# Two gated linear-attention blocks on one core: A's reciprocals spread through a DRAM scratch, and part of A's row work moved

## The chip, the core and the metric

The kernel runs on one core of one Trainium2 chip. A core has five engines that run side by side, each with its own queue of instructions that it works through in order: TensorE (PE, matrix products, with a weight load before each matmul, shown as PEld), VectorE (DVE), ScalarE (ACT), GpSimd (POOL) and SyncE (SP, which here issues transfers). Matmuls write to PSUM, a small memory of eight banks per partition; everything else lies in SBUF, 128 partitions wide, or in DRAM. An engine that needs another's result waits on a semaphore, and what is queued behind the waiting instruction waits too.

The metric is the time of one execution on the device in microseconds, lower is better.

## The reference

The input x has 2048 rows of 640 features. Two attention blocks, A and B, with weights of their own work on the same x, and a gate mixes them:

```
qkv = x @ wqkv                        # 640 -> 3 * 640; 32 heads of 20 features
phi = lambda t: where(t > 0, t + 1, exp(t)) + 1e-6
pq, pk = phi(q), phi(k)
kv  = einsum("bhsd,bhse->bhde", pk, v)
z   = einsum("bhsd->bhd", pk)
num = einsum("bhqd,bhde->bhqe", pq, kv)
den = einsum("bhqd,bhd->bhq", pq, z)[..., None] + 1e-6
o   = num / den ;  block = o @ wo
g   = sigmoid((x * gate_w).sum(-1, keepdims=True))
out = g * A(x) + (1 - g) * B(x)
```

All inputs and the output are bf16.

## The kernel before

The kernel never forms v. Since kv = pk' x wv, it makes G = x' pk (640 x 640), multiplies it by the weights of v, keeps the blocks on the diagonal that belong to the same head, and multiplies by wo: the result is one matrix M for each block, and the output is pq_A M_A + pq_B M_B, if each row of pq is first multiplied, head by head, by gate / den.

The stages, in the order in which TensorE meets them (times of the profiled execution):

- k of A and half of A's q, then the other half of q (up to 52.7 us). A chunk of k has 128 rows, ten matmuls of 320 columns (`k_mm`, L210); a unit of q has 128 features and 1024 rows, ten matmuls of 512 columns (`q_unit`, L259). Behind each, `phi` (L197) takes an exp on ACT (L200), a min and add on DVE (L203) and an add and max on DVE (L207), which frees the PSUM bank pair. The q rows are kept transposed in `pqT[b]`, as five feature tiles of 128 partitions by 2048 rows; tile m holds every fifth feature from m on, so that partition p of each tile belongs to head p // 4.
- `g_all` (A from 52.7 to 74.1 us, B from 122.1 to 143.5 us): one feature tile of G by `g_pass`, the denominators and their reciprocals by `rec_pass`, and the other four tiles of G by a scheme of Strassen's kind (`g_strassen`, L323): seven products of 16 matmuls (`g_prod`, L318), in two PSUM bank pairs that are partly accumulated over and partly read out between the products by `add` (L335, L366).
- k of B (74.1 to 99.0 us) in 16 chunks, with A's kv and M_A (`kv_a`, `m_a`) between them. M_A's rows go to a DRAM scratch, `ma_dram`, and come back as one transfer on SP's queue. `p_diff` stands here too, after chunks 3, 6, 9 and 12: `D3` = first half of A's scaled q rows minus the second half, a quarter of the rows of all five tiles at a time, 128x1280 elements.
- q of B (99.0 to 122.1 us): ten units. Behind the fourth and behind the last stands a difference of pk rows (`k_sum(1, 1)`, `k_sum(1, 2)`, 128x2560 on DVE).
- `g_all` for B, then M_B and the output product, again in Strassen's manner, in eight pairs of row blocks (`Pair`), up to the end at 189.7 us. `D3` is read from 151.8 us on.

The reciprocals, in detail. `rec_pass` (L468) makes the denominators as a tile whose 128 partitions are 4 groups of 256 rows by 32 heads, for each half of the rows. DVE adds eps and multiplies by the gate (L477, 128x256) and takes the reciprocal (L482, 128x256) into `rT`, once for each half. The q rows want it with 4 partitions for each head and all 2048 rows along the free dimension. `norm_spread` (L518) does that with eight matmuls of a 0/1 matrix (`spread`, L524, four for each half) into two PSUM bank pairs, which ACT copies into `R` (L529, two copies). `scale(b, m)` (L534, L537) then multiplies feature tile m of `pqT[b]` by `R`, 128x2048 bf16 on DVE. In `g_strassen` the spreading stands behind the second product, and the five multiplications stand one or two at a time between the read-outs of the later products.

From `k_chunk(0, ST - 2)` on, the order of the instructions on each engine is the order in which the program writes them (`tc.manual_schedule()`); before that a scheduler sets it. The Tile framework adds the waits, by the regions that instructions read and write.

Of the kernel before, what the change touches and what calls it, by code (L numbers as in the profile page):

```python
# [8 lines left out]
P = 128  # L9
FP32 = mybir.dt.float32  # L10
BF16 = mybir.dt.bfloat16
ACT = mybir.ActivationFunctionType
ALU = mybir.AluOpType

S, D, H = 2048, 640, 32
# [7 lines left out]
TW = 4  # L23
# [5 lines left out]
RB = 256  # L29
SH = S // 2  # L30
# [3 lines left out]
def kernel(  # L34
# [11 lines left out]
    nc = tc.nc  # L46
# [7 lines left out]
    scratch = ctx.enter_context(tc.tile_pool(name="scratch", bufs=1, space=bass.MemoryType.DRAM))  # L54
# [12 lines left out]
    def ps(name, slot=None):  # L67

        return ps_raw(name, slot).bitcast(FP32).rearrange("p (b n) -> p b n", b=2)
# [4 lines left out]
    pqT = [persist.tile([P, DT, S], BF16, name=f"pqT{b}") for b in "AB"]  # L74
# [10 lines left out]
    R = persist.tile([P, 2, 4, RB], BF16, name="R")  # L85
    ones = persist.tile([P, H], BF16, name="ones")
    gwr = persist.tile([P, DT, H], BF16, name="gwr")
    D3 = persist.tile([P, DT, SH], BF16, name="D3")
    hc, ic = ST // 2, 2 * P

    def flat(t, pattern, inner, at=0):
        n = hc * inner
        return t[:].rearrange(pattern)[:, at * n:(at + 1) * n].rearrange("p (i n) -> p i n", i=hc)
# [4 lines left out]
    TK = [{k: flat(pqT[1], "p c s -> p (c s)", HF, k - 1) for k in (1, 2, 3, 4)},  # L98
          {k: flat(xT, "p c s -> p (c s)", HF, k - 2) for k in (2, 3, 4)}]
    ma_dram = scratch.tile([D, D], BF16, name="ma_dram")  # L100
    lift = persist.tile([P, 1], FP32, name="lift")
    TM = [persist.tile([P, DT, HF], BF16, name="TM0")] + [None] * 3
    ge = [persist.tile([P, 2 * RB], FP32, name=f"ge{b}") for b in "AB"]
# [30 lines left out]
    for n in range(1, NB):  # L134
        for c in range(DT):
            nc.sync.dma_start_transpose(
                out=xT[:, c, n * HB:(n + 1) * HB], in_=x2[n * HB:(n + 1) * HB, c * P:(c + 1) * P]
# [4 lines left out]
    for r in range(4):  # L142
        rows = slice(32 * r, 32 * r + 32)
        nc.gpsimd.tensor_copy(out=I4[rows], in_=ident[rows, rows])
    nc.gpsimd.tensor_copy(
        out=spread[:].rearrange("p (h t) -> p h t", t=TW), in_=I4[:, :, None].to_broadcast([P, H, TW])
    )
    nc.gpsimd.memset(maskE[:], 1.0)
    for sign, base in ((1, 0), (-1, Dh - 1)):
        nc.gpsimd.affine_select(  # L150
            out=maskE[:], in_=maskE[:], pattern=[[-sign * Dh, WB[0] // Dh], [0, Dh]],
# [3 lines left out]
    for r in range(4):  # L155
        rows = slice(32 * r, 32 * r + 32)
        for sign, base in ((1, 0), (-1, Dh - 1)):
            nc.gpsimd.affine_select(
                out=E4[rows], in_=E4[rows], pattern=[[sign, D]],
# [121 lines left out]
    def g_pass(b, c, slot):  # L281

        pt = ps(f"g{'AB'[b]}", slot)
        for i in range(ST):
            for hf in range(2):
                g_mm(c, i, hf, pt)
        for hf in range(2):
            nc.scalar.copy(out=GT[hf][:, c, :], in_=pt[:, hf, 0:HF])
# [17 lines left out]
    def k_sum(b, k):  # L306

        b11, b12 = [pk[:, 0:hc, n * HF:(n + 1) * HF] for n in range(2)]
        b21, b22 = [pk[:, hc:ST, n * HF:(n + 1) * HF] for n in range(2)]
        t = TK[b]  # L310
        left, right = {1: lambda: (b12, b11), 2: lambda: (b22, t[1]), 3: lambda: (b22, b12), 4: lambda: (b21, t[2])}[k]()
        add_rows(t[k], left, right, ALU.subtract)

    def g_prod(pt, left, right, first):

        for i in range(hc):
            for n in range(2):
                nc.tensor.matmul(  # L318
                    pt[:, n, 0:HF], lhsT=left[:, i, n * P:(n + 1) * P], rhs=right[:, i, :],
                    start=(first and i == 0), stop=(i == hc - 1), skip_group_check=not first,  # L320
                )

    def g_strassen(b, norm):  # L323

        x11, x12 = [xn[:, k:k + hc, 0:ic] for k in (0, hc)]
        x22 = xn[:, hc:ST, ic:2 * ic]
        b11 = pk[:, 0:hc, 0:HF]
        b21, b22 = [pk[:, hc:ST, n * HF:(n + 1) * HF] for n in range(2)]
        lo, hi = GT

        def temp(name):
            return work.tile([P, 2, HF], FP32, tag="osb", name=name, bufs=3)

        def add(dst, pt, sb):
            nc.vector.tensor_tensor(out=dst, in0=pt[:, :, 0:HF], in1=sb[:], op=ALU.add)  # L335

        even, odd = ps("gs0", 0), ps("gs1", 1)
        g_prod(even, x11, b11, True)
        p1 = temp("p1")
        nc.scalar.copy(out=p1[:], in_=even[:, :, 0:HF])  # L340
        g_prod(odd, SX[2], TK[b][2], True)
        u2 = temp("u2")
        add(u2[:], odd, p1)
        k_sum(b, 4)
        norm()
        g_prod(even, x12, b21, False)
        nc.scalar.copy(out=lo[:, 0:2, :], in_=even[:, :, 0:HF])
        scale(b, 0)
        scale(b, 1)
        g_prod(odd, SX[3], TK[b][3], False)  # L350
        u3 = temp("u3")
        add(u3[:], odd, p1)
        if b == 0:
            x_sum(4)
        else:
            scale(b, 2)
        even = ps("gs0", 0)
        g_prod(even, SX[1], TK[b][1], True)
        add(hi[:, 2:4, :], even, u3)
        scale(b, 3 if b else 2)  # L360
        g_prod(odd, x22, TK[b][4], False)
        add(lo[:, 2:4, :], odd, p1)
        scale(b, 4 if b else 3)
        g_prod(even, SX[4], b22, False)
        for n in range(2):
            nc.vector.tensor_tensor(out=hi[:, n, :], in0=even[:, n, 0:HF], in1=u2[:, n], op=ALU.add)  # L366
        if b == 0:
            scale(b, 4)

    def z_rows(b):  # L370

# [96 lines left out]
    def rec_pass(b, zsel, slot):  # L468

        pt = ps(f"den{'AB'[b]}", slot)  # L470
        for h in range(2):
            by_group(pt[:, 0, h * RB:(h + 1) * RB], zsel, pqT[b], h)
        rts = []
        for h in range(2):
            part = slice(h * RB, (h + 1) * RB)
            d1 = work.tile([P, RB], FP32, tag="d1", name="d1", bufs=1)
            nc.vector.scalar_tensor_tensor(  # L477
                out=d1[:], in0=pt[:, 0, part], scalar=EPS, in1=ge[b][:, part], op0=ALU.add, op1=ALU.mult
            )
            rT = work.tile([P, RB], BF16, tag="rT", name="rT")  # L480
            with nc.allow_low_precision(reason="a fp32 reciprocal, stored as the bf16 that multiplies bf16"):
                nc.vector.reciprocal(out=rT[:], in_=d1[:])  # L482
            rts.append(rT)
        return rts

    def add_rows(dst, a, b, op):
        nc.vector.tensor_tensor(out=dst, in0=a, in1=b, op=op)  # L487

    def p_diff(rows):

        up = slice(SH + rows.start, SH + rows.stop)
        add_rows(D3[:, :, rows], pqT[0][:, :, rows], pqT[0][:, :, up], ALU.subtract)

    def p_sums(rows, ks=(1, 2, 4)):

# [22 lines left out]
    def norm_spread(b, rts, slots):  # L518

        pts = [ps(f"ex{'AB'[b]}", s) for s in slots]  # L520
        for h in range(2):
            for j in range(4):
                rows = slice(32 * j, 32 * j + 32)
                nc.tensor.matmul(  # L524
                    pts[j // 2][:, j % 2, h * RB:(h + 1) * RB], lhsT=spread[rows, :], rhs=rts[h][rows, :],
                    start=True, stop=True,
                )
        for jj in range(2):
            nc.scalar.copy(  # L529
                out=R[:, :, 2 * jj:2 * jj + 2, :].rearrange("p h j n -> p j h n"),  # L530
                in_=pts[jj][:].rearrange("p j (h n) -> p j h n", n=RB),
            )

    def scale(b, m):  # L534

        rec = R[:].rearrange("p h j n -> p (h j n)")
        nc.vector.tensor_tensor(out=pqT[b][:, m, :], in0=pqT[b][:, m, :], in1=rec, op=ALU.mult)  # L537
# [106 lines left out]
    def q_pass(b, units):  # L644

        units = list(units)
        q_unit(b, *units.pop(0))
        if b == 0:
            gate_pass()
        zr = z_rows(b)  # L650
        for k in range(2):
            if b == 0:
                x_sum(1 + k)
            q_unit(b, *units.pop(0), b == 0)
        zsel = z_pass(b, zr)
        for k, (m, h) in enumerate(units):
            if b == 0 and k < 2:
                if k:
                    x_sum(3)
                else:  # L660
                    k_sum(0, 2)
            q_unit(b, m, h, b == 0)
            if b == 1 and k == 0:
                k_sum(1, 1)
        if b == 1:
            k_sum(1, 2)
        return zsel

    def g_all(b, zsel):

        g_pass(b, DT - 1, 1)
        k_sum(b, 3)
        rts = rec_pass(b, zsel, 2)
        g_strassen(b, lambda: norm_spread(b, rts, (2, 3)))


    with tc.manual_schedule():
# [12 lines left out]
    for n in range(1, NB):  # L690
        nc.sync.dma_start(
            out=xn[:, n * CB:(n + 1) * CB, :], in_=x2[n * HB:(n + 1) * HB, :].rearrange("(q p) d -> p q d", p=P)
# [11 lines left out]
    with tc.manual_schedule():  # L704
# [10 lines left out]
        for i in range(ST):  # L715
            k_chunk(1, i)
            if i > 3 and i % 2 == 0:
                m_a(i // 2 - 2)
            if i == 1:
                kv_a()  # L720
                wv[1] = load_w(1, "v", nc.sync)
            if i in (3, 6, 9, 12):
                r0 = (i - 3) // 3 * RB
                p_diff(slice(r0, r0 + RB))
        load_wo(1, nc.sync)
        t1 = wpool.tile([P, hc, HF], BF16, tag="wk", name="T1")
        TK[1][1] = t1[:]
# [109 lines left out]
```

## Time and profile before

| | |
|---|---|
| time, median of 3 runs | 190.9 us (190.49 to 191.43) |
| the profiled execution | 191.42 us, span 189.7 us |
| TensorE busy | 184.0 us, 97% of the span |
| VectorE busy | 152.7 us, 80% |
| ScalarE busy | 70.5 us, 37% |
| transfers | 15.63 MB, mean 82 GB/s |
| a reciprocal (L482, 128x256) | 1.75 us, four of them |
| a multiplication by R (L537, 128x2048) | 1.22 us, ten of them |
| a difference of q rows into D3 (L487, 128x1280) | 0.815 us, four of them |
| an R copy from PSUM (L529, 128x1024) | 1.01 us, four of them |

The span is the time from the first to the last instruction of one execution that a hardware profiler recorded; the time of an execution is a little longer than its span. A line of the timeline gives the start, the duration, the engine, the line of the program, the operation with the tiles that it writes and reads, and the number of instructions merged into it; in brackets stands the idle time of the engine before it and what ended it. The chain of work that ended last is followed back from the last instruction, at each step to what released it. DVE's records overlap a little: the next instruction starts some 0.08 us before the listed end of the one in front.

### The profile page before, as it was taken

Reading aid. Unit: us, or ns where it says so; the run is one execution under the profiler, and the core shown is the slowest. Engines: PE = TensorE matmul, PEld = TensorE weight load, DVE = VectorE, ACT = ScalarE, POOL = GpSimd, SP = SyncE. Lnnn points to the kernel's source line nnn. Section 1 sums busy time; section 2 is a strip of 40 time slices with the busy share of each in tenths; the row PEclk is TensorE's granted clock in tenths of the full one; section 3 lists DMA queues with packets and bytes.
Section 4 is the critical chain, followed back from the end, with each engine's and each line's share of the span. In section 5 each row is a group of like instructions: output and inputs, shape, how many; then the busy total and the mean of one; then the engine's idle time right before and its main releaser. Section 6 shows DMA issues by size and latency. Waiting matters only on the chain.

```text
span 189.7 us, 3630 instructions
## 1 busy us (share of the span) xinstructions
PE 184.0 (97%) x1490; PEld 124.7 (66%) x1497; DVE 152.7 (80%) x244; ACT 70.5 (37%) x99; POOL 8.6 (5%) x23
## 2 busy tenths in 40 slices
PE   8799999999999999999999999999999999999992
PEld 3566657765567677877775555576777776777771
DVE  1378968899898999789886689799999989787553
ACT  2055446455953500357672445412401611111110
POOL 8900000000000000000000000000000000000000
PEclk9999999999999999999999999999999999999999
DMA  5976438993050000241116600000000003212112
GB/s 181 324 143 87 88 78 273 343 224 101 2 173 0 3 0 0 42 166 32 54 40 218 146 5 0 0 0 3 0 0 3 3 0 108 99 65 77 69 69 73
DMA packets 19802, 15.63 MB, mean 82 GB/s; under 512 B 9546, under 2 KB 19658, under 8 KB 19786
## 3 DMA queue, kind: packets, MB, share of 16 engines
q1 hardware_dynamic: 18922, 14.59, 28.5%
q10 hardware_dynamic: 864, 0.82, 1.3%
q8 instruction: 11, 0.18, 0.4%
q14 instruction: 5, 0.04, 0.1%
HBM read 10.00 MB, written 3.44 MB: 71 GB/s over the span
## 4 chain that ended last, share of the span: by engine, by line
PE 93%; DMA 3%; DVE 1%; ACTq 0%; issue 0%; ACT 0%; DVEq 0%
PE gs L318 16%; PE kB L210 11%; PE qB L259 11%; PE kA L210 11%; PE qA L259 7%; PE ox L548 6%; PE oy L548 5%; PE oz L548 5%; PE qA L270 4%; DMA xn<-in_A_x_dram 3%; PE ow L548 3%; PE gB L291 2%; PE gA L291 2%; DVE osb L553 1%; PE mA L441 1%; PE mid L402 1%
## 5 line engine op out<-in xcount | busy, mean ns | idle before, releaser
L210 PEld LDWEIGHTS <-xT 128*128 128x128 bf16 x320 | 31.0, 98 | 12.3 <-DVE xT L195 0.4
L203 DVE TENSOR_SCALAR e<-e 128x640 bf16<-128x640 bf16 (+1 forms) x52 | 18.8, 361 | 9.6 <-ACT e L200 9.0
L210 PE MATMUL kB<-wkB,xT 128*128 128x320 bf16 x160 | 23.0, 299 | 0.0
L210 PE MATMUL kA<-wkA,xT 128*128 128x320 bf16 x160 | 22.6, 299 | 0.0
L259 PE MATMUL qB<-xT,wqB 128*128 128x512 bf16 x97 | 22.0, 379 | 0.2
L200 ACT ACTIVATE e<-kB 128x640 bf16<-128x640 f32 x16 | 11.3, 704 | 18.8 <-PE kB L210 17.5
L259 PEld LDWEIGHTS <-wqB 128*128 128x128 bf16 x100 | 11.6, 118 | 9.6 <-issue 0.3
L200 ACT ACTIVATE e<-kA 128x640 bf16<-128x640 f32 x16 | 11.1, 704 | 13.6 <-PE kA L210 13.6
L200 ACT ACTIVATE e<-qB 128x1024 bf16<-128x1024 f32 x10 | 10.2, 1024 | 13.2 <-PE qB L259 10.7
L207 DVE SCALAR_TENSOR_TENSOR pk<-kA,e 128x640 bf16<-128x640 f32 x16 | 13.2, 824 | 1.7
L207 DVE SCALAR_TENSOR_TENSOR pk<-kB,e 128x640 bf16<-128x640 f32 x16 | 13.2, 824 | 1.7
L200 ACT ACTIVATE e<-qA 128x1024 bf16<-128x1024 f32 x10 | 10.2, 1024 | 10.6 <-PE qA L259 5.2
L259 PE MATMUL qA<-xT,wqA 128*128 128x512 bf16 x58 | 13.5, 380 | 0.1
L207 DVE SCALAR_TENSOR_TENSOR pqTB<-qB,e 128x1024 bf16<-128x1024 f32 x10 | 12.2, 1224 | 1.0
L318 PEld LDWEIGHTS <-S 128*128 128x128 bf16 x96 | 9.4, 98 | 3.6
L318 PEld LDWEIGHTS <-xn 128*128 128x128 bf16 x96 | 9.1, 98 | 4.0 <-issue 0.4
L592 ACT COPY u<-ox 128x320 f32<-128x320 f32 x8 | 3.4, 426 | 21.9 <-PE ox L548 21.9
L259 PEld LDWEIGHTS <-wqA 128*128 128x128 bf16 x60 | 6.9, 118 | 5.6 <-issue 0.3
L548 PEld LDWEIGHTS <-xT 128*128 128x128 bf16 x85 | 8.0, 98 | 3.1 <-DVE xT L487 0.2
L548 PEld LDWEIGHTS <-pqTA 128*128 128x128 bf16 x85 | 7.9, 98 | 2.9 <-issue 0.2
L548 PEld LDWEIGHTS <-pqTB 128*128 128x128 bf16 x80 | 7.8, 98 | 3.0
L576 ACT COPY p1s<-ox 128x320 f32<-128x320 f32 x8 | 3.4, 426 | 16.6 <-PE ox L548 16.6
(121 smaller groups left out, 287.7 us busy)
## 6 DMA issues: line engine op xcount, KB each, us to landing
out_dram<-osb SPq DMA_DIRECT2D x14, 160.0 KB, 1.8
xn<-in_A_x_dram SPq DMA_DIRECT2D x3, 640.0 KB, 7.2
wqA<-in_A_wqkv_dram SPq DMA_DIRECT2D x1, 800.0 KB, 6.5
wvA<-in_A_wqkv_dram SPq DMA_DIRECT2D x1, 800.0 KB, 11.0
wkB<-in_B_wqkv_dram SPq DMA_DIRECT2D x1, 800.0 KB, 5.8
wqB<-in_B_wqkv_dram SPq DMA_DIRECT2D x1, 800.0 KB, 4.5
wvB<-in_B_wqkv_dram SPq DMA_DIRECT2D x1, 800.0 KB, 4.6
MA<-ma_dram SPq DMA_DIRECT2D x1, 800.0 KB, 4.4
```

Of the source, the lines that this page charges most:

```text
L200: nc.scalar.activation(out=e[:], in_=src, func=ACT.Exp)
L203: nc.vector.tensor_scalar(e[:], e[:], 1.0, EPS, op0=ALU.min, op1=ALU.add)
L207: nc.vector.scalar_tensor_tensor(out=dst, in0=src, scalar=1.0 + EPS, in1=e[:], op0=ALU.add, op1=ALU.max)
L210: nc.tensor.matmul(pt[:, hf, 0:HF], lhsT=xT[:, c, i * P:(i + 1) * P], rhs=wk[b][:, c, hf * HF:(hf + 1) * HF], start=(c == 0), stop=(c == D ...
L259: nc.tensor.matmul(pt[:, u, :], lhsT=mixed(wq[b][:, c, :], m), rhs=xT[:, c, n * HB:(n + 1) * HB], start=(c == 0), stop=(c == DT - 1),)
L270: nc.tensor.matmul(pt[:, u, :], lhsT=mixed(wq[b][:, c, :], m + u), rhs=xT[:, c, n * HB:(n + 1) * HB], start=(c == 0), stop=(c == DT - 1),)
L291: nc.tensor.matmul(pt[:, hf, 0:HF], lhsT=xn[:, i, c * P:(c + 1) * P], rhs=pk[:, i, hf * HF:(hf + 1) * HF], start=(i == 0), stop=(i == ST - 1),
L318: nc.tensor.matmul(pt[:, n, 0:HF], lhsT=left[:, i, n * P:(n + 1) * P], rhs=right[:, i, :], start=(first and i == 0), stop=(i == hc - 1), s ...
L402: nc.tensor.matmul(pt[:KG, hf, j * KG:(j + 1) * KG], lhsT=wv[b][:, c, (4 * hf + j) * KG:(4 * hf + j + 1) * KG], rhs=GT[hf][:, c, j * KG:(j ...
L548: nc.tensor.matmul(dst, lhsT=left[:, c, r0:r0 + P], rhs=right[:, c, :], start=(first and c == 0), stop=(c == DT - 1), skip_group_check=not ...
L576: nc.scalar.copy(out=self.p1s[:], in_=self.at("x"))
L592: nc.scalar.copy(out=self.u2[:], in_=self.at("x"))
```

## The change

Four things are changed, all of them for block A's q rows; B's reciprocals are spread as before.

- A's reciprocals `rT` (128x256 bf16, two halves) are stored to a new DRAM scratch, `r_dram`, by SP's queue, as soon as each half is there. `norm_load` then loads `R` from it in four transfers, one for each partition of the four that belong to a head (32 partitions, 8 runs of 512 bytes in each). A's eight spreading matmuls and two PSUM copies go.
- In A's `g_strassen` the multiplications of tiles 0, 1 and 2 now stand where those of tiles 2, 3 and 4 stood; the place behind the fourth product, where 0 and 1 stood, is empty.
- The multiplications of A's tiles 3 and 4 stand in B's q pass, behind the sixth and the eighth of its ten units.
- `p_diff` takes one feature tile with all 1024 rows at a time (128x1024). Tiles 0, 1 and 2 stand in B's k chunks, behind chunks 4, 8 and 12; tiles 3 and 4 stand in B's q pass, behind the seventh and the ninth unit.

```diff
+    r_dram = scratch.tile([2, P, RB], BF16, name="r_dram")
...
         nc.scalar.copy(out=lo[:, 0:2, :], in_=even[:, :, 0:HF])
-        scale(b, 0)
-        scale(b, 1)
+        if b == 1:
+            scale(b, 0)
+            scale(b, 1)
...
-        scale(b, 3 if b else 2)
+        scale(b, 3 if b else 0)
         g_prod(odd, x22, TK[b][4], False)
         add(lo[:, 2:4, :], odd, p1)
-        scale(b, 4 if b else 3)
+        scale(b, 4 if b else 1)
...
         if b == 0:
-            scale(b, 4)
+            scale(b, 2)
...
             rts.append(rT)
+            if b == 0:
+                nc.sync.dma_start(out=r_dram[h], in_=rT[:])
...
-    def p_diff(rows):
-
-        up = slice(SH + rows.start, SH + rows.stop)
-        add_rows(D3[:, :, rows], pqT[0][:, :, rows], pqT[0][:, :, up], ALU.subtract)
+    def p_diff(c):
+
+        add_rows(D3[:, c, :], pqT[0][:, c, 0:SH], pqT[0][:, c, SH:S], ALU.subtract)
...
+    def norm_load():
+
+        src = r_dram[:].rearrange("a (j h) n -> h a j n", h=H)
+        for u in range(TW):
+            nc.sync.dma_start(out=R[u::TW], in_=src)
...
             q_unit(b, m, h, b == 0)
             if b == 1 and k == 0:
                 k_sum(1, 1)
+            if b == 1 and k in (2, 4):
+                scale(0, k // 2 + 2)
+            if b == 1 and k in (3, 5):
+                p_diff(k // 2 + 2)
...
         rts = rec_pass(b, zsel, 2)
-        g_strassen(b, lambda: norm_spread(b, rts, (2, 3)))
+        if b == 0:
+            norm_load()
+        g_strassen(b, lambda: norm_spread(b, rts, (2, 3)) if b else None)
...
-            if i in (3, 6, 9, 12):
-                r0 = (i - 3) // 3 * RB
-                p_diff(slice(r0, r0 + RB))
+            if i in (4, 8, 12):
+                p_diff(i // 4 - 1)
```

## The prediction

> **What bounds the kernel now.** I read the page first, for the engine shares and the chain of work that ended last; then that chain in order of time around the two places that the change touches; then VectorE's timeline there; then the waits, the DMA issues and the granted clock.
>
> The page's first part and its chain:
>
> ```profile
> PE 184.0 (97%) x1490; PEld 124.7 (66%) x1497; DVE 152.7 (80%) x244; ACT 70.5 (37%) x99; POOL 8.6 (5%) x23
> PE 93%; DMA 3%; DVE 1%; ACTq 0%; issue 0%; ACT 0%; DVEq 0%
> ```
>
> TensorE is the bound: 97% busy, 93% of the chain. A saving counts only if it takes time out of TensorE's queue, and a delay elsewhere counts as soon as TensorE waits for it. The chain in order of time where A's reciprocals are spread, and at the same place for B:
>
> ```profile
> 58.29 4.45 PE gs L318 x32
> 62.74 0.40 PE exA L524 x8
> 63.15 10.97 PE gs L318 x80
> ...
> 122.11 4.35 PE gB L291 x32
> 126.45 1.21 PE denB L174 x40
> 127.66 4.45 PE gs L318 x32
> 132.11 0.40 PE exB L524 x8
> 132.51 10.97 PE gs L318 x80
> ```
>
> The spreading matmuls (exA, exB) stand on the path for 0.40 us each. Only A's go. Now VectorE (DVE) in B's q pass and behind it, until B's reciprocals are done (columns: start us, duration us; in brackets the idle time before):
>
> ```profile
> 110.25 0.43 DVE L203 TENSOR_SCALAR e<-e 128x1024 bf16<-128x1024 bf16 x1 [0.37 <-ACT e L200]
> ...
> 118.88 0.43 DVE L203 TENSOR_SCALAR e<-e 128x1024 bf16<-128x1024 bf16 x1 [0.40 <-ACT e L200]
> ...
> 123.20 0.43 DVE L203 TENSOR_SCALAR e<-e 128x1024 bf16<-128x1024 bf16 x1 [0.40 <-ACT e L200]
> 123.73 1.22 DVE L207 SCALAR_TENSOR_TENSOR pqTB<-qB,e 128x1024 bf16<-128x1024 f32 x1
> 124.87 1.48 DVE L487 TENSOR_TENSOR xT<-pk,T 128x2560 bf16<-128x2560 bf16 x1
> 126.27 1.48 DVE L487 TENSOR_TENSOR xT<-pk 128x2560 bf16<-128x2560 bf16 x1
> 127.71 0.42 DVE L477 SCALAR_TENSOR_TENSOR d<-denB,geB 128x256 f32<-128x256 f32 x1
> 128.17 1.75 DVE L482 RECIPROCAL rT<-d 128x256 bf16<-128x256 f32 x1
> 129.96 0.42 DVE L477 SCALAR_TENSOR_TENSOR d<-denB,geB 128x256 f32<-128x256 f32 x1
> 130.41 1.75 DVE L482 RECIPROCAL rT<-d 128x256 bf16<-128x256 f32 x1
> ```
>
> What to see: from 123.20 to the second reciprocal's end (130.41 + 1.75 = 132.16) DVE runs without a gap worth naming, and exB, which needs that reciprocal, stands on TensorE at 132.11. The slack there is nil. Whatever DVE gets to do in B's q pass beyond its idle time ends up as a TensorE wait in front of exB's second half.
>
> **The change part by part.** Durations are of the profiled execution: span 189.7, time 191.42 us, at the upper end of the three runs (median 190.9). I make the sum as a difference and put it on the median.
>
> 1. *A's spreading matmuls go.* Eight matmuls, 0.40 us by the chain. Bounds: columns alone, at kB's rate (10 matmuls of 320 columns in 1.36 us), are 2 x 256 x 0.425 ns = 0.22 us, four row groups side by side; the whole stretch is 0.40. I take 0.40, since the stretch's waits go too. The two R copies on ACT (2 x 1.01 us) also go; ACT waits for TensorE behind them (9.4 us before its next exp), so they are worth nothing.
>
> 2. *A's R by DRAM.* Two stores of 64 KB and four loads of 128 KB on SP's queue. SP issues nothing between 52.8 and 78.4 us (weights wqB, then wvB) and DMA is idle there, so nothing is queued behind them that suffers: wvB still waits for TensorE's kvA. The second store waits for the reciprocal that ends at 62.80. A store of this kind to the scratch and the dependent load behind it took 1.76 us (the last evacuation of M_A's rows ends at 98.68, the load of MA is issued at 100.44), so the R loads issue from 64.6, at 0.35 us each. Landing, lower end by bytes: MA and woB, issued one behind the other, brought 1,600 KB in 7.6 us, so 512 KB in 2.5: 67.1. Upper end by packets: gcol, 640 packets, took 4.9 us; 1,024 packets of 512 B then take 7.8: 72.4. I take 69, nearest the byte end, because these packets are like those of the weights. [...]
>
> 3. *Three multiplications (L537) later in A's Strassen product, two of them moved on.* On DVE, u3 and SX4 now come without two multiplications in front, so nothing there is later. The first multiplication comes behind the add that in the old trace starts at 69.81; shifted by 0.40 and with 0.74 for the add, at 70.15. With R at 69 it waits for nothing. The multiplication behind the last add stands where it stood, so DVE enters B's k chunks with the same lag behind TensorE. Cost 0. If R is late, what waits behind the multiplication is the add into GT (0.82) that frees the bank of B's first k chunk, due at 73.55: TensorE is held from R > 73.55 - 0.82 - 1.14 = 71.6 on; at R = 72.4 the cost is 0.8 us.
>
> 4. *Differences by feature tile.* Four of 128x1280 (0.815 each) leave the k chunks, three of 128x1024 come in. At L205's 0.692 us for 128x1024 bf16 that is 1.2 us less DVE work in a stretch where TensorE never waits: worth nothing. The last two go to the q pass.
>
> 5. *B's q pass gets two multiplications and two differences.* DVE's instructions follow each other 0.08 us before the listed end (the 1.48 at 124.87 is followed at 126.27), so they cost 1.14 and 0.61 net: 2 x 1.14 + 2 x 0.61 = 3.50 us. DVE's idle time behind the first k_sum (from 113.32 on) is 0.07 before 116.72, three times 0.49 (118.88, 121.04, 123.20, measured from the follower's earliest start) and 0.04 before 127.71: 1.58. DVE is late by 3.50 - 1.58 = 1.92 us at the second reciprocal. Bounds: if the four cost the full listed time, 3.82 - 1.58 = 2.24; if only the idle that the trace calls idle (3 x 0.40) is kept out, 3.50 - 1.20 = 2.30; if the differences cost as little by the column as k_sum does (1.40 net for 2560, so 0.56) 1.82. I take 1.92, since it uses the duration of the same shape.
> What waits on the way: gB's first matmul needs the bank of the fifth of the last seven units, whose phi now ends at 121.83, against 122.11: no wait. denB's last four matmuls need the last unit's phi, now 126.91, against 127.5: no wait. The second Strassen product needs k_sum 2, now 128.3, against 129.77: no wait. exB's second four matmuls need the second reciprocal, now 132.16 + 1.92 = 134.08, and they would start at about 132.2: TensorE waits 1.9 us. Behind it both queues go on with their old distance, DVE meeting TensorE again at the add at 139.18, where it had 0.22 us idle.
>
> Sum: -0.40 + 0 + 0 + 0 + 1.92 = +1.5 us. On the profiled execution 192.9, on the median 192.4.
>
> The stall and the clock: the trace's own case of a stop is the end of the span, where TensorE stops at 186.2 and the granted clock holds 1.00 to 188.5 and then falls:
>
> ```profile
> 188.00:188.50 0.50, 0.00 (x0) 0.00 (x0) 0.00 (x0) 0.00 (x0) 0.00 (x0) 1.00 0.03 8
> 188.50:189.00 0.50, 0.00 (x0) 0.00 (x0) 0.00 (x0) 0.00 (x0) 0.00 (x0) 0.88 0.00 0
> 189.00:189.70 0.70, 0.00 (x0) 0.00 (x0) 0.00 (x0) 0.00 (x0) 0.00 (x0) 0.50 0.00 0
> ```
>
> (The next to last three columns are granted clock, DMA share, GB/s.) That is about 2.7 us of idleness; 1.9 is less, so no clock loss is in the sum. [...]
>
> **The rivals.**
> *Hidden after all (not slower).* DVE's four added instructions fit into its idle time, and exB waits for nothing. It decides where they cost at most 1.58 + 0.40 = 2.0 us together instead of 3.50. For it: DVE idles before each q unit. Against: the measured 1.22 and 0.69. Time: 190.9 - 0.4 = 190.5, within noise.
> [...]
> *The clock falls in the stall.* It decides if idleness of 1.9 us is enough. For as long as the old trace needed to fall (2.7 us) at 0.5, TensorE loses 1.35 us: 193.8. For it: the one drop came at 2.7, not far off. Against: TensorE idles 0.97 us at 6 us at clock 1.00.
>
> **How the numbers follow.** About 0.5% (0.95 us) is what a measurement of this kernel can tell from no change. Forecast 0.74, hidden 0.10, R late 0.09, clock 0.04, something else that gains 0.03. Of the forecast's share, the lower bound (1.82 - 0.4 = +1.4) and the spread of the runs (190.49 to 191.43) put about 0.08 within 0.5%. Slower: 0.66 + 0.09 + 0.04 = 0.79; same: 0.10 + 0.08 = 0.18; faster 0.03, since only 0.40 us is removed from the path. The time is 192.4. The forecast's own range is 191.9 to 193.2 (+1.4 to +1.9, and the runs' spread of about 0.4 below and above that); with R late at 193.2 and part of the way to the hidden case it is 191.3 to 193.4.
>
> **What would show it.** Right: no exA row; TensorE's idle time before exB (or the chain passing over DVE's reciprocal there) about 1.9 us; B's second reciprocal ending about 1.5 us later than 132.16; the first multiplication at about 70.2 with no wait on a DMA; k chunks 0.4 us earlier. Wrong: the second reciprocal less than 0.9 us late, R landing behind 71.6, a granted clock under 1.00 near 133, or a wait of TensorE that none of these steps names.

## The result, and the profile after

The changed kernel takes 192.46 us (median of 6 runs, 192.21 to 194.84), the kernel before 190.80 us beside it: a ratio of 1.0106 with a 95% interval of 1.0065 to 1.0146. It is slower by about 1.1%, and the forecast of 192.4 us holds. Its profiled execution took 192.37 us, with a span of 190.6 us.

The page's first part and the chain by engine, for the changed kernel:

```profile
PE 184.5 (97%) x1482; PEld 125.1 (66%) x1489; DVE 152.5 (80%) x245; ACT 68.6 (36%) x97; POOL 8.6 (5%) x23
PE 83%; DVE 13%; issue 1%; ACT 1%; DVEq 0%; ACTq 0%
```

The shares of busy time say nothing: 97% and 80%, as before. The chain does: VectorE had 1% of the path and now has 13%, because from B's q pass on the path runs over VectorE until B's reciprocals are done. The chain in order of time (start us, duration us, what), with the matmuls that now follow A's denominators without a break, and the end of the stretch that belongs to VectorE:

```profile
56.76 1.20 PE denA L175 x40
57.97 15.32 PE gs L319 x112
...
129.55 1.76 DVE rT L484
131.80 1.76 DVE rT L484
...
133.89 10.97 PE gs L319 x80
```

A's spreading matmuls are gone (112 matmuls in one piece). B's reciprocals stand on the path, and B's Strassen products go on at 133.89, against 132.51 before. What TensorE waited for there, from the timeline of the changed kernel:

```profile
131.80 1.75 DVE L484 RECIPROCAL rT<-d 128x256 bf16<-128x256 f32 x1
...
131.91 0.29 PE L527 MATMUL exB<-rT,spread 32*128 32x256 bf16 x4 [0.37 <-DVE d L479]
...
133.60 0.29 PE L527 MATMUL exB<-rT,spread 32*128 32x256 bf16 x4 [1.40 <-DVE rT L484]
```

The second half of B's spreading matmuls starts 0.05 us behind the end of the second reciprocal (131.80 + 1.75 = 133.55). TensorE is idle for 0.37 + 1.40 us there. On VectorE, in front of it, stand the four instructions of A (start, duration, and idle time before in brackets):

```profile
109.42 0.43 DVE L204 TENSOR_SCALAR e<-e 128x1024 bf16<-128x1024 bf16 x1 [0.37 <-ACT e L201]
110.31 1.22 DVE L208 SCALAR_TENSOR_TENSOR pqTB<-qB,e 128x1024 bf16<-128x1024 f32 x1 [0.47 <-DVE e L204]
...
116.18 1.22 DVE L546 TENSOR_TENSOR pqTA<-pqTA,R 128x2048 bf16<-128x2048 bf16 x1
117.31 0.42 DVE L204 TENSOR_SCALAR e<-e 128x1024 bf16<-128x1024 bf16 x1
...
118.98 0.68 DVE L491 TENSOR_TENSOR D<-pqTA 128x1024 bf16<-128x1024 bf16 x1
119.58 0.42 DVE L204 TENSOR_SCALAR e<-e 128x1024 bf16<-128x1024 bf16 x1
...
121.24 1.22 DVE L546 TENSOR_TENSOR pqTA<-pqTA,R 128x2048 bf16<-128x2048 bf16 x1
...
124.03 0.68 DVE L491 TENSOR_TENSOR D<-pqTA 128x1024 bf16<-128x1024 bf16 x1
```

From start to next start they cost 1.13 and 0.60 us, 3.46 in all, and no idle time is left behind them: the three gaps of 0.40 that the old trace had there have gone. The line at 110.31 shows something else: a pause of 0.36 us between the two steps of a phi (0.89 us from start to start, 0.53 in all its neighbours). It gets an experiment of its own below.

To compare kernels I use one stretch that start-up and the last stores don't touch: from the start of A's denominators in the chain (57.09 before, 56.76 after) to the restart of B's products (132.51 and 133.89). It is 75.42 us before and 77.13 us after, +1.71 us. The two profiled executions differ by 0.95 us only (191.42 and 192.37), because the one of the changed kernel had a start-up 0.33 us shorter and ended 2.7 us behind its last VectorE instruction instead of 3.2. The medians differ by 1.66.

### The profile page after: what moved, and what is told of

The parts are those of the page before. It is cut to its first block, busy times and chain, and to the rows that moved or that the text cites. A ratio compares the mean times of both kernels' runs of the same rounds, so it can differ in the third digit from the quotient of the medians.

```text
span 190.6 us, 3627 instructions
## 1 busy us (share of the span) xinstructions
PE 184.5 (97%) x1482; PEld 125.1 (66%) x1489; DVE 152.5 (80%) x245; ACT 68.6 (36%) x97; POOL 8.6 (5%) x23
## 4 chain that ended last, share of the span: by engine, by line
PE 83%; DVE 13%; issue 1%; ACT 1%; DVEq 0%; ACTq 0%
PE gs L319 14%; PE kA L211 12%; PE kB L211 11%; PE qA L260 7%; PE ox L557 6%; PE oy L557 5%; PE oz L557 5%; PE qB L260 5%; DVE pqTB L208 4%; PE qA L271 4%; PE ow L557 2%; PE gA L292 2%; DVE rT L484 2%; PE warm L168 2%; DVE e L204 1%; DVE xT L491 1%
## 5 line engine op out<-in xcount | busy, mean ns | idle before, releaser
L211 PE MATMUL kA<-wkA,xT 128*128 128x320 bf16 x160 | 23.4, 306 | 0.0
L201 ACT ACTIVATE e<-qB 128x1024 bf16<-128x1024 f32 x10 | 10.2, 1024 | 13.2 <-PE qB L260 10.7
L201 ACT ACTIVATE e<-qA 128x1024 bf16<-128x1024 f32 x10 | 10.2, 1024 | 10.6 <-PE qA L260 5.2
L319 PE MATMUL gs<-pk,xn 128*128 128x320 bf16 x64 | 9.4, 299 | 0.0
```

The lines of the kernel that those rows point to most:

```text
L201: nc.scalar.activation(out=e[:], in_=src, func=ACT.Exp)
L211: nc.tensor.matmul(pt[:, hf, 0:HF], lhsT=xT[:, c, i * P:(i + 1) * P], rhs=wk[b][:, c, hf * HF:(hf + 1) * HF], start=(c == 0), stop=(c == D ...
L319: nc.tensor.matmul(pt[:, n, 0:HF], lhsT=left[:, i, n * P:(n + 1) * P], rhs=right[:, i, :], start=(first and i == 0), stop=(i == hc - 1), s ...
```

## The experiments

The theory that the prediction rests on: VectorE's work in B's q pass, beyond its idle time there, reaches TensorE through B's second reciprocal (the surplus theory). The rival: the way of A's reciprocals through DRAM costs the time (the transfer theory). Each kernel is the changed kernel with the edit shown. A ratio is to the kernel before, measured beside it: that one took 190.84 us beside the first, second, third and fifth of the kernels below, 191.42 us beside the fourth, sixth and seventh, and 190.93 us beside the last. Medians of different experiments are therefore compared by their ratios. The finer sums rest on the stretch, which is read from one profiled execution of each kernel.

**The same work, ahead of the fourth unit of the q pass.**

```diff
         zr = z_rows(b)
+        if b == 1:
+            scale(0, 4)
         for k in range(2):
...
             q_unit(b, *units.pop(0), b == 0)
+            if b == 1:
+                p_diff(3 + k)
...
-            if b == 1 and k in (2, 4):
-                scale(0, k // 2 + 2)
-            if b == 1 and k in (3, 5):
-                p_diff(k // 2 + 2)
...
+        scale(0, 3)
         zsel = q_pass(1, [(m, h) for h in range(2) for m in range(DT)])
```

> The same four instructions for A's tiles 3 and 4, but ahead of the fourth unit of B's q pass, where VectorE idled about 3.0 us in all (1.22, 1.00, 0.40 and 0.37 before the first phi steps). Surplus theory (VectorE's work in the q pass beyond its idle time reaches TensorE through B's second reciprocal): 3.46 us of work meet 3.0 + 1.58 us of idleness, the second spreading matmuls wait no longer, and what is left is the saving of A's spreading matmuls: 190.8 - 0.5 = 190.3 us, ratio about 0.997. Transfer theory (the way through the DRAM scratch costs): no change against the changed kernel, 192.4 us. A theory that the amount of work counts and not its place: 192.4 us too.

Measured: 190.09 us, ratio 0.9952 (0.9932 to 0.9972). The stretch (56.68 to 131.60) is 74.92 us, 0.50 less than before. Its chain:

```profile
56.68 1.21 PE denA L175 x40
57.89 15.32 PE gs L319 x112
...
131.20 0.40 PE exB L527 x8
131.60 10.97 PE gs L319 x80
```

The spreading matmuls of B are back at 0.40 us in one piece, with no wait. The loss was in the place of four instructions, not in their amount, and the transfer theory falls: the transfers are all there. This version is faster than both kernels, than the one before by about 0.5%.

**A's reciprocals spread by matmuls again, the moved work left in place.**

```diff
             rts.append(rT)
-            if b == 0:
-                nc.sync.dma_start(out=r_dram[h], in_=rT[:])
...
-        if b == 0:
-            norm_load()
-        g_strassen(b, lambda: norm_spread(b, rts, (2, 3)) if b else None)
+        g_strassen(b, lambda: norm_spread(b, rts, (2, 3)))
```

> The changed kernel with A's reciprocals spread by matmuls and PSUM copies again, no DRAM scratch, all moved work left where the change put it. Surplus theory: the loss stays and A's spreading matmuls come back on the path, 192.4 + 0.5 = 192.9 us, ratio about 1.011. Transfer theory: the loss goes, 190.8 us, ratio 1.000.

Measured: 193.53 us, ratio 1.0135 (1.0088 to 1.0183). Without the transfers the loss stays, so it is not in them. The stretch (56.52 to 133.80) is 77.28 us, +1.86. Three of its six runs took 192.5 to 192.8 us, at a mean granted clock of 0.997 or more, and three took 194.3 to 195.0 us at 0.990 or 0.991. The first three are about as slow as the changed kernel; the 0.5 us that I had expected on top is 0.15 in the stretch (77.28 against 77.13), since the pause of 0.36 us is absent here. The profiled execution is one of the latter. Its granted clock behind the wait (windows in us; the last three columns are granted clock, DMA share, GB/s), and the chain's entry of the products there:

```profile
133.00:133.50 0.50, 0.00 (x0) 0.00 (x0) 0.50 (x2) 0.00 (x0) 0.00 (x0) 1.00 0.00 0
...
134.00:134.50 0.50, 0.50 (x6) 0.37 (x4) 0.50 (x2) 0.50 (x1) 0.00 (x0) 1.00 0.00 0
134.50:135.00 0.50, 0.50 (x5) 0.36 (x4) 0.50 (x1) 0.50 (x2) 0.00 (x0) 0.79 0.00 0
135.00:135.50 0.50, 0.50 (x4) 0.27 (x3) 0.50 (x1) 0.50 (x1) 0.00 (x0) 0.50 0.00 0
...
138.00:139.00 1.00, 1.00 (x8) 0.69 (x7) 0.15 (x1) 0.00 (x0) 0.00 (x0) 0.90 0.00 0
```

```profile
133.80 12.65 PE gs L319 x80
```

TensorE restarted at 133.51 and 133.74, and about 1.1 us later, at 134.79, the clock was halved, until 138.2 (both moments worked out from the mean of their window). The 80 matmuls took 12.65 us instead of 10.97: 1.68 us more. So the rival of the falling clock is real, in some executions.

**One tile late, one early.**

```diff
             q_unit(b, *units.pop(0), b == 0)
+            if b == 1 and k == 0:
+                p_diff(3)
...
-            if b == 1 and k in (2, 4):
-                scale(0, k // 2 + 2)
-            if b == 1 and k in (3, 5):
-                p_diff(k // 2 + 2)
+            if b == 1 and k == 4:
+                scale(0, 4)
+            if b == 1 and k == 5:
+                p_diff(4)
...
+        scale(0, 3)
         zsel = q_pass(1, [(m, h) for h in range(2) for m in range(DT)])
```

> Half the dose: only tile 4's multiplication and difference stay late in B's q pass (1.73 us net); tile 3's go ahead of the fourth unit. Surplus theory with its threshold: 1.73 against 1.58 us idle is 0.15 us too much, so 190.8 - 0.5 + 0.2 = 190.5 us, ratio 0.998; not halfway. A cost in proportion to the work moved late (no threshold) would give about 190.3 + 1.05 = 191.4 us. Transfer theory: 192.4 us.

Measured: 190.77 us, ratio 0.9997 (0.9978 to 1.0017), stretch 75.61 (56.43 to 132.04), +0.19. The ratio alone does not exclude the 0.998 that I had expected, but the stretch gives neither of my numbers: the loss is 0.69 us (0.19 + 0.50), not 0.15, and not the 1.05 of a cost in proportion. From its timeline:

```profile
117.72 0.43 DVE L204 TENSOR_SCALAR e<-e 128x1024 bf16<-128x1024 bf16 x1 [0.40 <-ACT e L201]
118.25 1.23 DVE L208 SCALAR_TENSOR_TENSOR pqTB<-qB,e 128x1024 bf16<-128x1024 f32 x1
119.39 1.22 DVE L546 TENSOR_TENSOR pqTA<-pqTA,R 128x2048 bf16<-128x2048 bf16 x1
120.52 0.42 DVE L204 TENSOR_SCALAR e<-e 128x1024 bf16<-128x1024 bf16 x1
...
122.18 0.68 DVE L491 TENSOR_TENSOR D<-pqTA 128x1024 bf16<-128x1024 bf16 x1
```

```profile
131.75 0.29 PE L527 MATMUL exB<-rT,spread 32*128 32x256 bf16 x4 [0.59 <-DVE rT L484]
```

VectorE still idles at 117.72, ahead of the moved multiplication. That idle time is lost: the multiplication stands behind these two instructions in VectorE's queue and starts at 119.39, with no wait of its own. Only the gaps behind the moved work count, 2 x 0.49 + 0.04 = 1.02 us, and 1.73 - 1.02 = 0.71 us go through, against 0.69 measured. In the changed kernel all the idle time that the prediction counted stood behind the first moved instruction, and VectorE was late at each of these gaps, so the prediction's sum held there. I carried the same 1.58 us over to one tile moved further back, and there it was wrong. My theory needed this correction, and the next experiment tests it.

**The same one tile, behind the last unit.** As above, but tile 4's two instructions stand here:

```diff
-            if b == 1 and k == 4:
-                scale(0, 4)
-            if b == 1 and k == 5:
-                p_diff(4)
         if b == 1:
+            scale(0, 4)
+            p_diff(4)
             k_sum(1, 2)
```

> As the kernel with one tile late, but tile 4's multiplication and difference stand behind the last unit of B's q pass instead of behind its eighth and ninth unit: the same 1.73 us of work, with only 0.04 us of VectorE idleness left behind it instead of 1.02. Queue theory (only the idleness that comes behind the moved work counts): 1.69 us reach TensorE, 190.8 - 0.5 + 1.7 = 192.0 us, ratio 1.006, against 190.77 us for the kernel with one tile late. Plain sum theory (work against all 1.58 us of idleness of the pass): 190.5 us, no different from the other.

Measured: 192.04 us, ratio 1.0030 (1.0005 to 1.0055). The stretch (57.13 to 133.87) is 76.74 us, +1.32, where the corrected theory gives -0.50 + 1.69 = 1.19. TensorE's wait, and the two moved instructions on VectorE:

```profile
131.88 0.29 PE L527 MATMUL exB<-rT,spread 32*128 32x256 bf16 x4 [0.24 <-DVE d L479]
...
133.58 0.29 PE L527 MATMUL exB<-rT,spread 32*128 32x256 bf16 x4 [1.40 <-DVE rT L484]
```

```profile
124.41 1.22 DVE L546 TENSOR_TENSOR pqTA<-pqTA,R 128x2048 bf16<-128x2048 bf16 x1
125.66 0.69 DVE L491 TENSOR_TENSOR D<-pqTA 128x1024 bf16<-128x1024 bf16 x1
```

The same 1.73 us of work cost 0.69 us in its places one and two units earlier, and costs 1.82 here (1.32 + 0.50). The missing 0.13 us: the difference now stands right behind the multiplication whose output it reads, and starts 1.25 us behind its start instead of 1.13. The ratios alone tell less: this one's interval begins at 1.0005, and that of the other place ends at 1.0017. The ratio of 1.006 that I had expected lies just outside of this one's interval. That the median met the expected 192.0 us is chance, for the kernel before took 191.42 us beside it and not 190.8.

**Work taken from in front of the reciprocals.** Nothing removed; B's third difference of pk rows goes behind them:

```diff
+        if b == 1:
+            k_sum(b, 3)
         k_sum(b, 4)
         norm()
...
-        k_sum(b, 3)
+        if b == 0:
+            k_sum(b, 3)
         rts = rec_pass(b, zsel, 2)
```

> The changed kernel with B's third difference of pk rows (1.40 us net on VectorE) moved from ahead of B's reciprocals to behind them; no work is taken away. Surplus theory: the second reciprocal ends 1.4 us earlier (132.2 instead of 133.6), the wait of the spreading matmuls shrinks by as much, 192.4 - 1.4 = 191.0 us, ratio 1.001. Transfer theory, or a loss that comes from the sum of VectorE's work: 192.4 us.

Measured: 190.77 us, ratio 0.9986 (0.9962 to 1.0009), a little below the 1.001 that I had expected; stretch 75.73 (57.68 to 133.41), +0.31, which is 1.40 less than the changed kernel's, as expected.

```profile
133.12 0.29 PE L529 MATMUL exB<-rT,spread 32*128 32x256 bf16 x4 [0.44 <-DVE rT L486]
```

The wait behind the reciprocal shrinks from 1.40 to 0.44. What counts is what stands in VectorE's queue ahead of the reciprocals, whatever it is.

**Both tiles last, and TensorE kept busy in the wait.** The first of two kernels puts both tiles' instructions behind the last unit; the second adds matmuls without use in B's spreading (the first hunk), whose output is overwritten:

```diff
         for h in range(2):
+            for n in range((14, 12)[h]):
+                nc.tensor.matmul(pts[1][:, 1, RB:2 * RB], lhsT=spread[:], rhs=one_r[:, 0:RB], start=True, stop=True)
             for j in range(4):
...
-            if b == 1 and k in (2, 4):
-                scale(0, k // 2 + 2)
-            if b == 1 and k in (3, 5):
-                p_diff(k // 2 + 2)
         if b == 1:
+            for m in (3, 4):
+                scale(0, m)
+                p_diff(m)
             k_sum(1, 2)
```

> Both tiles' four instructions behind the last unit of B's q pass: 3.46 us with no idleness behind. Queue theory: 190.8 - 0.5 + 3.4 = 193.7 us with the clock held; if TensorE's wait, now about 3.4 us with a short stretch of four matmuls in it, makes the granted clock fall to 0.50 for about 3.4 us as it did in one profile of the kernel with the spreading matmuls back, 1.7 us more, 195.4 us, in most executions. Plain sum theory: 192.4 us as the changed kernel.

> The kernel with both tiles last, and 26 matmuls of 256 columns without use (14 ahead of B's spreading matmuls, 12 between their halves) that fill TensorE's waits there with about 2.8 us of work; their output is overwritten. If TensorE's idleness is what lowers the clock, the granted clock stays at 1.00 in all executions and the time is 193.7 us, the same as both tiles last with the clock held (up to 0.3 us more where the fill runs over). If the clock falls for another reason, it falls here as often as there.

Measured: 195.35 us (1.0199, 1.0157 to 1.0242) and 194.16 us (1.0139, 1.0110 to 1.0168). The stretch is 78.60 us, +3.18, in both profiles (56.53 to 135.13 and 57.46 to 136.06): -0.50 + 3.42, and twice the 0.12 of a difference right behind its multiplication. The pause of 0.36 us does not add to it, since here idle time of VectorE follows it. The idle kernel's six runs have mean granted clocks of 0.999, 0.991, 0.983, 0.991, 0.989 and 0.982; its profile is the first of them, at 193.57 us, the one execution of the six without the fall. Its waits:

```profile
133.15 0.29 PE L527 MATMUL exB<-rT,spread 32*128 32x256 bf16 x4 [1.73 <-DVE d L479]
...
134.84 0.29 PE L527 MATMUL exB<-rT,spread 32*128 32x256 bf16 x4 [1.40 <-DVE rT L484]
```

The busy kernel's six all have 1.00. Its TensorE timeline:

```profile
132.18 1.72 PE L526 MATMUL exB<-const-bfloat16-1.0,spread 128*128 128x256 bf16 x14
...
133.98 0.29 PE L529 MATMUL exB<-rT,spread 32*128 32x256 bf16 x4
134.20 1.50 PE L526 MATMUL exB<-const-bfloat16-1.0,spread 128*128 128x256 bf16 x12
...
135.77 0.29 PE L529 MATMUL exB<-rT,spread 32*128 32x256 bf16 x4
```

The wait is as long in both; only TensorE's idleness in it differs, and with it the fall of the clock. So it is the idleness that lowers the clock, and here it makes 1.2 us in the median.

**The pause in phi.** One VectorE instruction without use, earlier:

```diff
+            if i == 2:
+                nc.vector.memset(lift[:], 1.0 + EPS)
             if i in (4, 8, 12):
                 p_diff(i // 4 - 1)
```

> The changed kernel with one more VectorE instruction without use, a memset of 128x1 in B's k chunks (about 0.06 us in a stretch where VectorE has idleness), so that every later VectorE instruction stands one place further on in its stream. In the profile of the changed kernel VectorE paused 0.36 us between the two steps of phi of B's fourth q unit, though nothing that they need was late; kernels with other VectorE streams in front did not show it. If the pause hangs on the place in the instruction stream, it is gone or elsewhere here, and if it stands where idleness absorbs it, the stretch from A's denominators to B's fourth Strassen product gets 0.36 us shorter; the time is 192.1 us against 192.4. If the pause hangs on the instruction or the time, it stays at the fourth unit.

Measured: 192.25 us, ratio 1.0050 (1.0023 to 1.0077). The stretch (57.86 to 134.63) is 76.77 us, +1.35 and 0.36 less than the changed kernel's. The profiled execution (194.93 us) is one of two of the eleven at a mean clock of 0.991; its clock falls at 135.66, behind the stretch. The two steps of the fourth unit's phi:

```profile
110.51 0.43 DVE L204 TENSOR_SCALAR e<-e 128x1024 bf16<-128x1024 bf16 x1 [0.37 <-ACT e L201]
111.04 1.23 DVE L208 SCALAR_TENSOR_TENSOR pqTB<-qB,e 128x1024 bf16<-128x1024 f32 x1
```

The pause is gone (0.53 us from start to start). The changed kernel, the one with k_sum behind the reciprocals and the two with both tiles last, all four with the same number of VectorE instructions up to this place (137 in the profile) and the same transfers, show the pause at the same instruction. The kernels with one or more additional VectorE instructions ahead (138 to 141) don't. But neither does the one with A's matmul spreading, which also has 137; its multiplications wait for ScalarE's copies and not for transfers, and no run shows whether that is the reason. So the count of instructions alone does not decide it, there is one profile of each kernel, and what the pause is stays open.

## Why the prediction was right, and where it was off

All terms against the stretch of +1.71 us, by the prediction's own steps. The sum forecast +1.5 us. That 192.46 us came so close to 192.4 is luck in part: the misses of -0.10, -0.04 and +0.36 us below make the stretch 0.2 us longer than forecast, and the kernel before took 190.80 us beside it instead of 190.9.

1. *A's spreading matmuls go*: -0.40 predicted, -0.50 measured (the version with the work early, which differs from the kernel before by little else on the path; 77.28 against 76.77 between the kernel with them and the one without the pause gives 0.51). The chain books 0.40 us for them, but the products in front take 4.45 us with them behind and 4.38 without (32 of the 112 matmuls of 15.32 us): part of their price stood in another entry.

2. *R by DRAM*: 0 predicted, 0 measured, and R at 69 predicted. The four loads, from the transfers' answer for R and the timeline:

```profile
L541 SPq DMA_DIRECT2D R<-r_dram x4: 597/608/697, 64.3 to 66.3; - x4
...
DMA to landing us min/median/max: 2.7/2.8/3.0
```

```profile
69.72 1.21 DVE L546 TENSOR_TENSOR pqTA<-pqTA,R 128x2048 bf16<-128x2048 bf16 x1
```

The last is issued at 66.3 and lands 2.7 to 3.0 us later, at 69.0 to 69.3, and the first multiplication starts at 69.72 with no wait. The landing was right by luck in part: an issue took 0.6 us, not the 0.35 of MA's, so the last load was issued later than assumed and landed faster after its issue. The margin is 0.4 us only up to the multiplication. Up to TensorE it is about 1.4 more, by the prediction's way of counting it: B's first k chunk starts at 73.12, and 73.12 - 0.82 - 1.14 = 71.16, against 69.72. Each of the four landed within 3.0 us of its own issue, and they were issued about 0.66 us apart, so they were under way together.

3. and 4. *The multiplications and differences that stayed in A's products and B's k chunks*: 0 predicted, 0 measured; between 57.97 and 100 us TensorE waits for nothing on VectorE or the transfers, and the version with the work early gains the full 0.50.

5. *Four instructions in B's q pass*: 3.50 - 1.58 = 1.92 predicted. Measured 3.46 for the work, so 1.88 through; the kernel with the spreading back, which has neither the gain nor the pause, shows +1.86. The place was right: the second reciprocal, and TensorE in front of the second half of exB. The sum fits this placement because all of the 1.58 us stands behind the first moved instruction. The rule that the prediction states (work in B's q pass "beyond its idle time") has no such condition, and the one-tile kernels showed that it is needed.

What the prediction did not have: the pause of 0.36 us, which goes straight through since no idle time is left behind it. It also made the wait at gB that the prediction had excluded with 0.28 us to spare: the bank came free at 121.32 and the weight load in front of gB idled for 0.38 us. (In the kernel without the pause gB starts 0.27 us earlier within the stretch.) That wait shortens the later one at exB and adds nothing. The sum of the measured terms is -0.50 + 1.88 + 0.36 = +1.74, against +1.71.

The rivals: *hidden after all* is what the version with the work early does, and what the change could have been. *R late* (0.09; +0.8 us at R = 72.4, by step 3) did not show: the last load had landed by 69.3. *The clock falls in the stall* was given 0.04 as a case against the forecast; it is a part of the executions instead, one of the changed kernel's six (194.84 us at 0.991), so that the median does not show it. The prediction held that 1.9 us of idleness is too little, from the one drop in the old trace, 2.7 us after TensorE's last work. That comparison was wrong: it took the idle time as a threshold. Of the prediction's own signs of being wrong, two showed in part: a wait of TensorE that none of its steps names, and a granted clock below 1.00, in one execution of six.

## What to carry to other kernels

An engine at 80% has idle time, but only the idle time that stands between the new work and the next instruction that the bounding engine waits for can take it in; idle time ahead of the work is lost, as the same 1.73 us of work showed by costing 0.69 us in one place and 1.82 in another. So ask for each moved instruction which queue it lengthens, find the next point where the bounding engine meets that queue, and count from there backwards. Moving the work ahead of the fourth unit, or moving other work behind that point, was worth 2.2 us (0.36 of it the pause, which is absent there) and 1.4 us of the stretch here, more than the 0.50 us that the change takes out of TensorE's queue.

## What the runs showed of the hardware that I had not expected

**The granted clock can fall after less than 2 us of idleness.** With TensorE idle for 1.6 to 1.8 us in front of exB, broken by four matmuls, it fell (mean clock 0.991 or less) in 3 of 6 runs of the kernel with the spreading back, in 1 of 6 of the changed kernel, in 1 of 12 with one tile last and in 2 of 11 with one more instruction; with about 3.1 us (1.73 + 1.40), in 5 of 6; with the same wait filled, in 0 of 6; with the work early, in 0 of 12. In the profile of the kernel with the spreading back it falls about 1.1 us after the restart, to 0.50, for 3.4 us (134.79 to 138.2), and costs 1.68 us. The profile of the kernel with one more instruction shows the same: a mean clock of 0.83 between 135 and 136 us, which puts the fall at 135.66, 1.1 us after its products restarted (134.56), then 0.50 up to 139 at least, and 12.65 us for the 80 matmuls. The 1.68 us that these are above 10.97 make, at half the clock, an estimated 3.4 us of low clock. How much idleness is safe was not shown: 1.7 us in front of exB was enough for a fall in these two profiles, while one execution with 3.1 us kept a mean clock of 0.999. Nor was it shown why only some executions fall.

**A pause of 0.36 us on VectorE that one more instruction ahead of it removed.** One additional instruction of 0.06 us ahead of it made the kernel's measured stretch 0.36 us shorter. It showed in four kernels at the same instruction, but not in every kernel with the same number of VectorE instructions ahead. Whether it has to do with how instructions are brought to the engine was not tried.
